# mLSTM cell and a cosine-gated MLP on one core: the model dimension cut into 128, 128 and 64 rows, and what comes with it

## The chip, the cores and the metric

The kernel runs on one core of one Trainium2 chip. A core has five engines that this text names as the profile does: PE (TensorE, matrix multiplication; PEld is its weight load), DVE (VectorE), ACT (ScalarE), POOL (GpSimd) and SP (SyncE, which here only issues DMAs). Each engine works through its own queue in order. The metric is the device time of one execution in microseconds; lower is better.

## What is computed

An mLSTM cell over 4 batches, 8 heads, 768 time steps and head dimension 40, and then an MLP of 320 to 2048 to 320 whose activation is h cos h. Cut to its core:

```python
for t in range(S):                     # batch b, head h
    m_new  = maximum(f[t] + m, i[t])
    f_stab = exp(f[t] + m - m_new); i_stab = exp(i[t] - m_new); m = m_new
    C = f_stab * C + i_stab * outer(v[t], k[t])
    n = f_stab * n + i_stab * k[t]
    y[t] = sigmoid(o[t]) * (C @ q[t]) / maximum(abs(n @ q[t]), 1.0)
x = y.transpose(0, 2, 1, 3).reshape(B * S, H * D)      # 3072 x 320
h = x @ w_in                                           # 320 -> 2048
out = (h * cos(h)) @ w_out                             # 2048 -> 320
```

The inputs q, k, v and the gates are float32. The two weight matrices arrive as float64 and are used as float32.

## The kernel before, in words

Time is cut into 6 blocks (c) of 128 steps. The running maximum m is made up front for all blocks by scans (lines 143 to 173), so that within a block the cell is matmuls. There are 24 **steps** n = 4c + b, one for each block and batch b. A step is `cell(n)` (line 198) and the loads for step n + 3:

- queries and keys are transposed (pt, line 211) and copied from PSUM by ACT and DVE (line 213, `t`);
- the decay matrix E comes by DMA as a row broadcast, DVE subtracts and clamps it head by head (line 218), ACT takes the exponential (line 220);
- scores ps (line 226): heads lie in pairs, one on partitions 0 to 39 and one on 64 to 103, and the first loop does the four even heads, the second the four odd ones; DVE multiplies by E (line 228);
- ph (line 232) is E times the values, with a column of ones for n; pq (line 237) is the query times the state; DVE joins them (hs, lines 240 and 241);
- dn (lines 245 to 247) is the denominator, and two DVE products (249, 250) turn the sigmoid of the output gate, in place, into y; a column scale of 2 pi is taken into dn;
- the state st is updated from pu (lines 254 to 268; POOL makes kw);
- y is transposed (px, line 276) into xT (lines 277 and 280), 320 rows as 120 + 120 + 80.

The MLP runs by block, over the 512 tokens of four batches. `up(c, f)` (line 285) makes one of 16 column blocks of 128: three matmuls (line 289, contraction over 120, 120 and 80 rows) into one of two PSUM banks (`pup`); ACT makes n, the nearest integer of h/2pi + 1/4, by writing int32 (line 293), and h (line 295); DVE takes the difference r straight from PSUM (line 297); ACT takes the sine (line 298); POOL multiplies g = h r (line 300). `down(c, b)` (line 303) sums 16 matmuls over g into po, ACT copies it (line 308) and SP stores it. g has 20 buffers; n, h and r have three each.

The weights are converted in 28 pieces by `to_float32` (line 109): SP fetches the bits, ACT makes the low bits and the absolute high word (118, 120), DVE clamps, shifts and joins the sign (121, 123, 125), POOL adds (126). `weights_in` makes 12 pieces before and between the first four steps (8 of 120 x 512, 4 of 80 x 512); `weights_out` makes 16 pieces of 128 x 320 during the up of block 0. `bits` has three buffers.

The order in the program is: load three steps; four steps with weights_in; then for each block c, four times (four up columns, one step of block c + 1), then four times down. A scheduler reorders each engine's queue within the dependences, so that up, cell and the next block's first up appear interleaved.

PSUM has eight banks: three for `ps_a` (pt, ph, pq, pu, px share them), two for ps, two for pup, one for po.

Of the kernel before, what the change touches and what calls it, by code (L numbers as in the profile page):

```python
# [3 lines left out]

# [7 lines left out]
FP = mybir.dt.float32  # L12
I32 = mybir.dt.int32
U32 = mybir.dt.uint32
AF = mybir.ActivationFunctionType
OP = mybir.AluOpType

LEAST, GREATEST = (struct.unpack("f", struct.pack("I", b))[0] for b in (0x38000000, 0x47EFFFFF))  # L20
TOP2 = -(1 << 30)

TWO_PI = 2.0 * math.pi

TWO_PI_DOWN = 6.28318500518798828125


@with_exitstack
def kernel(
# [20 lines left out]
    nc = tc.nc  # L50

    B, H, S, D = q.shape
    C = 128
# [4 lines left out]
    DM = H * D  # L58
    DFF = moe_w_in.shape[1]
    NF = DFF // 128  # L60

    KH = 3
    cuts = [(h * D, min(h + KH, H) * D) for h in range(0, H, KH)]
    KD = KH * D
    full = DM // KD
    NK = len(cuts)
    NB = 3

    const = ctx.enter_context(tc.tile_pool(name="const", bufs=1))
    wp = ctx.enter_context(tc.tile_pool(name="wp", bufs=1))  # L70
    p2 = ctx.enter_context(tc.tile_pool(name="p2", bufs=2))
    p3 = ctx.enter_context(tc.tile_pool(name="p3", bufs=3))
    dram = ctx.enter_context(tc.tile_pool(name="dram", bufs=1, space=bass.MemoryType.DRAM))
    ps_a = ctx.enter_context(tc.tile_pool(name="ps_a", bufs=3, space=bass.MemoryType.PSUM))
    ps_s = ctx.enter_context(tc.tile_pool(name="ps_s", bufs=1, space=bass.MemoryType.PSUM))
    ps_u = ctx.enter_context(tc.tile_pool(name="ps_u", bufs=2, space=bass.MemoryType.PSUM))
    ps_o = ctx.enter_context(tc.tile_pool(name="ps_o", bufs=1, space=bass.MemoryType.PSUM))


    ident = const.tile([128, 128], FP, name="ident")  # L80
# [2 lines left out]
    nc.gpsimd.memset(late, 0.0)  # L83
    nc.gpsimd.affine_select(out=late, in_=late, compare_op=OP.is_ge, fill=1.0e30, base=0,
                            pattern=[[1, C]], channel_multiplier=-1)
    one = const.tile([BH, 1], FP, name="one")
    nc.vector.memset(one, 1.0)

# [10 lines left out]
    for t in st:  # L99
        nc.gpsimd.memset(t, 0.0)  # L100

    w_in_sb = wp.tile([KD, NK, DFF], FP, name="w_in_sb")
    w_out_sb = wp.tile([128, NF, DM], FP, name="w_out_sb")


    WP = 512
    w_in_bits, w_out_bits = (w.bitcast(I32).rearrange("r (n two) -> r n two", two=2) for w in (moe_w_in, moe_w_out))

    def to_float32(dst, src, eng):
        rows, n = dst.shape  # L110
        r = slice(0, rows)
        bits = p3.tile([128, WP, 2], I32, name="bits", tag="bits")
        eng.dma_start(out=bits[r, 0:n], in_=src)
        hi, lo = bits[r, 0:n, 1], bits[r, 0:n, 0].bitcast(U32)
        t = p2.tile([128, WP], I32, name="wt", tag="wt")[r, 0:n]
        m = p2.tile([128, WP], I32, name="wm", tag="wm")[r, 0:n]

        nc.scalar.activation(out=m, in_=lo, func=AF.Copy, scale=2.0 ** -29)

        nc.scalar.activation(out=t.bitcast(FP), in_=hi.bitcast(FP), func=AF.Abs)  # L120
        nc.vector.tensor_scalar(out=t.bitcast(FP), in0=t.bitcast(FP), scalar1=LEAST, scalar2=GREATEST,  # L121
                                op0=OP.max, op1=OP.min)
        nc.vector.tensor_scalar(out=t, in0=t, scalar1=5, scalar2=2, op0=OP.logical_shift_left,
                                op1=OP.logical_shift_right)
        nc.vector.scalar_tensor_tensor(out=t, in0=hi, scalar=TOP2, in1=t, op0=OP.bitwise_and, op1=OP.bitwise_or)  # L125
        nc.gpsimd.tensor_tensor(out=dst.bitcast(I32), in0=t, in1=m, op=OP.add)

    def weights_in(f):
        for i, (lo, hi) in enumerate(cuts):
            to_float32(w_in_sb[0:hi - lo, i, ts(f, WP)], w_in_bits[lo:hi, ts(f, WP)], nc.sync)  # L130

    def weights_out(f):
        to_float32(w_out_sb[:, f], w_out_bits[ts(f, 128)], nc.sync)


    aT = const.tile([128, NC, BH], FP, name="aT")
# [6 lines left out]
    with tc.tile_pool(name="gates", bufs=1) as gates:  # L143
        f_sb = gates.tile([BH, S], FP, name="f_sb")
        nc.sync.dma_start(out=f_sb, in_=f_gate.rearrange("b h s -> (b h) s"))
        a = gates.tile([BH, S], FP, name="a")
# [31 lines left out]
    sig, xT = {}, {}  # L178
# [19 lines left out]
    def cell(n):  # L198
# [42 lines left out]
            nc.vector.tensor_tensor(out=hs, in0=hs, in1=ph, op=OP.add)  # L241

        dn = p2.tile([128, H], FP, name="dn", tag="dn")

        nc.vector.tensor_scalar(out=dn, in0=hs[:, :, D], scalar1=-TWO_PI, scalar2=TWO_PI, op0=OP.mult, op1=OP.max)
        nc.vector.scalar_tensor_tensor(out=dn, in0=hs[:, :, D], scalar=TWO_PI, in1=dn, op0=OP.mult, op1=OP.max)  # L246
        nc.vector.reciprocal(out=dn, in_=dn)
        y = sig[c][:, b]
        nc.vector.tensor_tensor(out=y, in0=y, in1=hs[:, :, 0:D], op=OP.mult)
        nc.vector.tensor_tensor(out=y, in0=y, in1=dn.unsqueeze(2).to_broadcast([128, H, D]), op=OP.mult)  # L250

        if c < NC - 1:
            kw = p2.tile([128, H, 64], FP, name="kw", tag="kw")
# [15 lines left out]


        if b == 0:
            xT[c] = p2.tile([KD, NK, B, C], FP, name="xT", tag="xT")
        px = ps_a.tile([KD, NK, C], FP, name="px", tag="a")
        yf = y.rearrange("p h d -> p (h d)")
        for i, (lo, hi) in enumerate(cuts):
            nc.tensor.transpose(px[0:hi - lo, i], yf[:, lo:hi], ident)  # L276
        nc.scalar.copy(out=xT[c][:, 0:full, b], in_=px[:, 0:full])  # L277
        for i in range(full, NK):
            r = slice(0, cuts[i][1] - cuts[i][0])
            nc.scalar.copy(out=xT[c][r, i, b], in_=px[r, i])  # L280


    gs = {}

    def up(c, f):
        pu = ps_u.tile([128, B * C], FP, name="pup", tag="up")
        for i, (lo, hi) in enumerate(cuts):
            r = slice(0, hi - lo)
            nc.tensor.matmul(pu, w_in_sb[r, i, ts(f, 128)], xT[c][r, i].rearrange("p b t -> p (b t)"),  # L289
                             start=(i == 0), stop=(i == NK - 1))  # L290

        n = p3.tile([128, B * C], I32, name="n", tag="n")
        nc.scalar.activation(out=n, in_=pu, func=AF.Copy, bias=0.25)  # L293
        h = p3.tile([128, B * C], FP, name="h", tag="h")
        nc.scalar.activation(out=h, in_=pu, func=AF.Copy, scale=TWO_PI)  # L295
        r = p3.tile([128, B * C], FP, name="r", tag="r")
        nc.vector.scalar_tensor_tensor(out=r, in0=pu, scalar=0.25, in1=n, op0=OP.add, op1=OP.subtract)  # L297
        nc.scalar.activation(out=r, in_=r, func=AF.Sin, scale=TWO_PI_DOWN)  # L298
        g = gp.tile([128, B * C], FP, name="g", tag="g")
        nc.gpsimd.tensor_tensor(out=g, in0=h, in1=r, op=OP.mult)  # L300
        gs[c, f] = g
# [24 lines left out]
    for n in range(max(B, NW)):  # L326
        if n < NW:
            weights_in(n)
        if n < B:
            step(n)  # L330
    for c in range(NC):
        for b in range(B):
            for f in range(b * NF // B, (b + 1) * NF // B):
                up(c, f)
                if c == 0:
                    weights_out(f)
            if c + 1 < NC:
                step((c + 1) * B + b)
        for b in range(B):
            down(c, b)  # L340
# [30 lines left out]
```

## Time and profile before

| | |
|---|---|
| median of three runs | 742.99 us (742.42 to 745.64) |
| profiled execution | 742.42 us, of it 740.1 us from the first to the last instruction |
| PE busy | 657.0 us (89%), 2714 matmul instructions |
| PEld busy | 427.9 us (58%) |
| DVE busy | 328.6 us (44%) |
| ACT busy | 316.5 us (43%) |
| POOL busy | 221.9 us (30%) |
| mean granted TensorE clock | 0.977 of full speed |

In the profile a line "L289 PE MATMUL pup<-xT,w_in_sb" names the line of the program, the engine, the operation, and what is written from what. Behind the bar stand the busy time, the mean of one in ns, and the idle time of the engine just before, with what ended it. A float32 matmul of the program is two matmul instructions in the profile. Durations of neighbours on one engine overlap where the engine pipelines them.

### The profile page before, as it was taken

How to read it: one execution, taken by the hardware profiler on the slowest of the kernel's cores; microseconds unless marked ns; L12 is line 12 of the kernel's file. 1: busy time of each engine (PE TensorE's matmuls, PEld its weight loads, DVE VectorE, ACT ScalarE, POOL GpSimd, SP SyncE). 2: the span in 40 equal slices, each digit the busy share in tenths (PEclk: the TensorE clock that was granted, in tenths of full speed). 3: DMA queues.
4: the chain of work that ended last, by engine and by line, in shares of the span. 5: the costliest groups of instructions: out<-in, count | busy, mean ns of one | idle time of the engine just before them, and what ended most of it. 6: DMA issues, size and time to landing. Idle time of an engine off the chain costs nothing.

```text
span 740.1 us, 7672 instructions
## 1 busy us (share of the span) xinstructions
PE 657.0 (89%) x2714; PEld 427.9 (58%) x2714; DVE 328.6 (44%) x726; ACT 316.5 (43%) x529; POOL 221.9 (30%) x213
## 2 busy tenths in 40 slices
PE   4075679889999999999999999999999999999998
PEld 3064545537665555665565665556765566664465
DVE  4178887896601666502656502665402444002200
ACT  4163346863524555433544423555223634026600
POOL 8023455453312333502323502333102322004400
PEclk9999998996999999999989999999899999999999
DMA  9797763341211222311212311211201100000000
GB/s 129 101 210 159 145 171 99 72 127 38 65 46 26 50 52 56 84 34 27 56 39 55 85 34 27 56 50 46 62 18 27 37 1 1 18 19 0 1 18 18
DMA packets 65244, 43.60 MB, mean 59 GB/s; under 512 B 53176, under 2 KB 57208, under 8 KB 65208
## 3 DMA queue, kind: packets, MB, share of 16 engines
q1 hardware_dynamic: 62088, 35.17, 20.3%
q0 software_dynamic: 3072, 7.87, 5.6%
q8 instruction: 21, 0.34, 0.2%
q14 instruction: 15, 0.12, 0.1%
q10 hardware_dynamic: 48, 0.10, 0.0%
HBM read 39.09 MB, written 4.03 MB: 58 GB/s over the span
## 4 chain that ended last, share of the span: by engine, by line
PE 73%; DVE 16%; issue 6%; ACT 3%; DMA 2%; POOL 0%; SPq 0%; DVEq 0%; ACTq 0%
PE po L306 27%; PE pup L289 25%; PE ph L232 8%; PE ps L226 4%; PE pu L257 3%; DVE E L218 3%; PE pq L237 3%; DVE dn L246 3%; PE pt L211 2%; DVE E L228 2%; DVE o L250 1%; PE px L276 1%; DVE st L268 1%; DVE wt L125 1%; DVE wt L121 1%
## 5 line engine op out<-in xcount | busy, mean ns | idle before, releaser
L289 PE MATMUL pup<-xT,w_in_sb 120*128 120x512 f32 (+1 forms) x576 | 269.5, 610 | 4.8 <-DVE r L297 4.8
L300 POOL TENSOR_TENSOR g<-h,r 128x512 f32<-128x512 f32 x96 | 122.8, 1284 | 330.0 <-ACT r L298 312.9
L306 PE MATMUL po<-w_out_sb,g 128*128 128x320 f32 x768 | 216.0, 435 | 2.5 <-ACT o_sb L308 1.5
L306 PEld LDWEIGHTS po<-w_out_sb,g 128*128 128x128 f32 x768 | 144.4, 191 | 67.0 <-ACT o_sb L308 10.2
L289 PEld LDWEIGHTS pup<-xT,w_in_sb 120*128 120x128 f32 (+1 forms) x576 | 107.7, 195 | 121.2 <-issue 97.1
L297 DVE SCALAR_TENSOR_TENSOR r<-pup,n 128x512 f32<-128x512 f32 x96 | 65.7, 687 | 214.0 <-ACT h L295 212.9
L293 ACT ACTIVATE n<-pup 128x512 int32<-128x512 f32 x96 | 57.0, 594 | 109.1 <-PE pup L289 107.0
L218 DVE SCALAR_TENSOR_TENSOR E<-E,aT,late 128x128 f32<-128x128 f32 x192 | 78.6, 470 | 23.2 <-DMA E<-M_d 23.2
L232 PE MATMUL ph<-vs,E 128*128 128x41 f32 x384 | 61.6, 318 | 27.3 <-issue 21.8
L232 PEld LDWEIGHTS ph<-vs,E 128*128 128x128 f32 x384 | 58.2, 231 | 35.0 <-issue 23.7
L298 ACT ACTIVATE r<-r 128x512 f32<-128x512 f32 x96 | 59.8, 635 | 42.4 <-DVE r L297 42.1
L308 ACT COPY o_sb<-po 128x320 f32<-128x320 f32 x24 | 10.2, 424 | 139.5 <-PE po L306 122.8
L295 ACT ACTIVATE h<-pup 128x512 f32<-128x512 f32 x96 | 56.9, 593 | 0.0
L226 PEld LDWEIGHTS ps<-t,t 40*128 40x128 f32 x384 | 42.8, 216 | 23.9 <-ACT t L213 10.4
L226 PE MATMUL ps<-t,t 40*128 40x128 f32 x384 | 47.7, 316 | 8.9 <-DVE t L213 6.8
L193 POOL DMA_DIRECT2D vs<-in_v_dram x24 | 22.1, 923 | 101.6 <-PE pu L257 90.6
L228 DVE TENSOR_TENSOR E<-ps,E 128x512 f32<-128x512 f32 x48 | 31.3, 687 | 22.4 <-PE ps L226 22.3
L276 PE MATMUL px<-ident,o 128*120 128x128 f32 (+1 forms) x72 | 13.6, 303 | 27.9 <-DVE o L250 27.9
L213 DVE COPY t<-pt 128x512 f32<-128x512 f32 x24 | 16.6, 690 | 47.6 <-PE pt L211 47.6
L277 ACT COPY xT<-px 120x256 f32<-120x256 f32 x24 | 8.8, 368 | 53.8 <-PE px L276 53.6
L220 ACT ACT_TABLE_LOAD x20 | 25.7, 1283 | 14.0 <-DMA E<-M_d 13.7
L276 PEld LDWEIGHTS px<-ident,o 128*120 128x120 f32 (+1 forms) x72 | 8.2, 141 | 40.6 <-issue 31.6
(65 smaller groups left out, 531.8 us busy)
## 6 DMA issues: line engine op xcount, KB each, us to landing
E<-M_d SPq DMA_DIRECT2D x24, 512.0 KB, 3.8
bits<-in_moe_w_out_dram SPq DMA_DIRECT2D x16, 320.0 KB, 3.3
qs<-in_q_dram SPq DMA_DIRECT2D x24, 160.0 KB, 3.2
ks<-in_k_dram SPq DMA_DIRECT2D x24, 160.0 KB, 3.5
vs<-in_v_dram POOLq DMA_DIRECT2D x24, 160.0 KB, 3.8
o<-in_o_gate_dram POOLq DMA_DIRECT2D x24, 160.0 KB, 4.2
bits<-in_moe_w_in_dram SPq DMA_DIRECT2D x8, 480.0 KB, 5.8
out_dram<-o_sb SPq DMA_DIRECT2D x24, 160.0 KB, 1.8
```

The source lines that it names most:

```text
L218: nc.vector.scalar_tensor_tensor(out=E[:, h], in0=E[:, h], scalar=aT[:, c, b * H + h:b * H + h + 1], in1=late, op0=OP.subtract, op1=OP.max)
L226: nc.tensor.matmul(ps[:, p], kT[r, p], qT[r, p], start=True, stop=True)
L228: nc.vector.tensor_tensor(out=w, in0=ps, in1=w, op=OP.mult)
L232: nc.tensor.matmul(ph[:, h], E[:, h], vs[i][:, h], start=True, stop=True)
L276: nc.tensor.transpose(px[0:hi - lo, i], yf[:, lo:hi], ident)
L289: nc.tensor.matmul(pu, w_in_sb[r, i, ts(f, 128)], xT[c][r, i].rearrange("p b t -> p (b t)"), start=(i == 0), stop=(i == NK - 1))
L293: nc.scalar.activation(out=n, in_=pu, func=AF.Copy, bias=0.25)
L295: nc.scalar.activation(out=h, in_=pu, func=AF.Copy, scale=TWO_PI)
L297: nc.vector.scalar_tensor_tensor(out=r, in0=pu, scalar=0.25, in1=n, op0=OP.add, op1=OP.subtract)
L298: nc.scalar.activation(out=r, in_=r, func=AF.Sin, scale=TWO_PI_DOWN)
L300: nc.gpsimd.tensor_tensor(out=g, in0=h, in1=r, op=OP.mult)
L306: nc.tensor.matmul(po, gs[c, f][:, ts(b, C)], w_out_sb[:, f], start=(f == 0), stop=(f == NF - 1))
```

## The change

- **Contraction.** The 320 rows are cut into 128, 128 and 64. `up` makes two column blocks at once: four matmuls over 128 rows, then two over 64 rows, the one on partitions 0 to 63, the other on 64 to 127. For that the last 64 rows of w_in are stored twice as narrow (`w_in_l`: even column blocks on the lower half, odd ones on the upper), and y carries its last 64 columns twice, so that px (now three whole transposes) puts them on both halves.
- **PSUM.** ps_a has two banks (three before), pup three (two before).
- **Activation.** h is copied from PSUM; n is rounded by adding and subtracting a large constant on ACT; DVE subtracts 2 pi n from h in two parts and clamps; ACT takes the absolute value and sin(pi/2 - |r|). Three ACT operations become five, one DVE operation becomes three, and DVE reads SBUF instead of PSUM.
- **Denominator.** The scale of 2 pi is gone; y is a tile of its own instead of the gate's.
- **Weights.** The conversion takes exponent, sign and mantissa apart: seven DVE operations a piece instead of three on DVE and two on ACT; the fetch is issued by POOL instead of SP. The pieces are 10 of 128 x 512 and 16 of 128 x 320; those of w_in_l are fetched by two DMAs.

```diff
-    ps_a = ctx.enter_context(tc.tile_pool(name="ps_a", bufs=3, space=bass.MemoryType.PSUM))
+    ps_a = ctx.enter_context(tc.tile_pool(name="ps_a", bufs=2, space=bass.MemoryType.PSUM))
...
-    ps_u = ctx.enter_context(tc.tile_pool(name="ps_u", bufs=2, space=bass.MemoryType.PSUM))
+    ps_u = ctx.enter_context(tc.tile_pool(name="ps_u", bufs=3, space=bass.MemoryType.PSUM))
...
-        eng.dma_start(out=bits[r, 0:n], in_=src)
+        for part, s in src:
+            eng.dma_start(out=bits[part, 0:n], in_=s)
...
-        nc.scalar.activation(out=m, in_=lo, func=AF.Copy, scale=2.0 ** -29)
-
-        nc.scalar.activation(out=t.bitcast(FP), in_=hi.bitcast(FP), func=AF.Abs)
-        nc.vector.tensor_scalar(out=t.bitcast(FP), in0=t.bitcast(FP), scalar1=LEAST, scalar2=GREATEST,
-                                op0=OP.max, op1=OP.min)
-        nc.vector.tensor_scalar(out=t, in0=t, scalar1=5, scalar2=2, op0=OP.logical_shift_left,
-                                op1=OP.logical_shift_right)
-        nc.vector.scalar_tensor_tensor(out=t, in0=hi, scalar=TOP2, in1=t, op0=OP.bitwise_and, op1=OP.bitwise_or)
-        nc.gpsimd.tensor_tensor(out=dst.bitcast(I32), in0=t, in1=m, op=OP.add)
+        nc.vector.tensor_scalar(out=t, in0=hi, scalar1=20, scalar2=0x7FF, op0=OP.logical_shift_right,
+                                op1=OP.bitwise_and)
+        nc.vector.tensor_scalar(out=t, in0=t, scalar1=float(REBIAS), scalar2=float(REBIAS + 254), op0=OP.max, op1=OP.min)
+        nc.vector.tensor_scalar(out=t, in0=t, scalar1=float(REBIAS), scalar2=float(1 << 23), op0=OP.subtract, op1=OP.mult)
+        nc.vector.scalar_tensor_tensor(out=t, in0=hi, scalar=SIGN, in1=t, op0=OP.bitwise_and, op1=OP.bitwise_or)
+
+        nc.vector.tensor_scalar(out=m, in0=hi, scalar1=TOP, scalar2=3, op0=OP.bitwise_and, op1=OP.logical_shift_left)
+        nc.vector.tensor_tensor(out=m, in0=m, in1=t, op=OP.bitwise_or)
+        t, m = t.bitcast(FP), m.bitcast(FP)
+        nc.vector.scalar_tensor_tensor(out=t, in0=lo, scalar=2.0 ** -52, in1=t, op0=OP.mult, op1=OP.mult)
+        nc.gpsimd.tensor_tensor(out=dst, in0=m, in1=t, op=OP.add)
...
-        nc.vector.tensor_tensor(out=y, in0=y, in1=dn.unsqueeze(2).to_broadcast([128, H, D]), op=OP.mult)
+        y = p2.tile([128, 2 * DM - KL], FP, name="y", tag="y")
+        yh = y[:, 0:DM].rearrange("p (h d) -> p h d", h=H)
+        nc.vector.tensor_tensor(out=yh, in0=sig[c][:, b], in1=hs[:, :, 0:D], op=OP.mult)
+        nc.vector.tensor_tensor(out=yh, in0=yh, in1=dn.unsqueeze(2).to_broadcast([128, H, D]), op=OP.mult)
+        nc.vector.tensor_copy(out=y[:, DM:], in_=y[:, KL:DM])
...
+        px = ps_a.tile([128, NK + 1, C], FP, name="px", tag="a")
+        for i in range(NK + 1):
+            nc.tensor.transpose(px[:, i], y[:, ts(i, 128)], ident)
+        nc.scalar.copy(out=xT[c][:, :, b], in_=px)
...
+        for e, pu in enumerate(pair):
+            for i in range(NK):
+                nc.tensor.matmul(pu, w_in_sb[:, i, ts(2 * f2 + e, 128)], x(i), start=(i == 0), stop=False)
+        for e, pu in enumerate(pair):
+            r = slice(64 * e, 64 * e + 64)
+            nc.tensor.matmul(pu, w_in_l[r, f2], x(NK, r), start=False, stop=True)
+        for e, pu in enumerate(pair):
+            act(c, 2 * f2 + e, pu)
...
-        n = p3.tile([128, B * C], I32, name="n", tag="n")
-        nc.scalar.activation(out=n, in_=pu, func=AF.Copy, bias=0.25)
         h = p3.tile([128, B * C], FP, name="h", tag="h")
-        nc.scalar.activation(out=h, in_=pu, func=AF.Copy, scale=TWO_PI)
+        nc.scalar.copy(out=h, in_=pu)
+        n = p3.tile([128, B * C], FP, name="n", tag="n")
+        nc.scalar.activation(out=n, in_=h, func=AF.Identity, scale=INV_2PI, bias=magic)
+        nc.scalar.activation(out=n, in_=n, func=AF.Identity, bias=unmagic)
         r = p3.tile([128, B * C], FP, name="r", tag="r")
-        nc.vector.scalar_tensor_tensor(out=r, in0=pu, scalar=0.25, in1=n, op0=OP.add, op1=OP.subtract)
-        nc.scalar.activation(out=r, in_=r, func=AF.Sin, scale=TWO_PI_DOWN)
+        nc.vector.scalar_tensor_tensor(out=r, in0=n, scalar=-TWO_PI_HI, in1=h, op0=OP.mult, op1=OP.add)
+        nc.vector.scalar_tensor_tensor(out=r, in0=n, scalar=-TWO_PI_LO, in1=r, op0=OP.mult, op1=OP.add)
+        nc.vector.tensor_scalar(out=r, in0=r, scalar1=math.pi, scalar2=-math.pi, op0=OP.min, op1=OP.max)
+        nc.scalar.activation(out=r, in_=r, func=AF.Abs)
+        nc.scalar.activation(out=r, in_=r, func=AF.Sin, scale=-1.0, bias=half_pi)
```

In the changed kernel the 128-row matmuls of up stand in line 308, the 64-row ones in line 311, the three DVE operations in lines 323 to 325, and the weights in lines 128 to 138.

## The prediction

> **What bounds the kernel now.** I read the page from the top: the busy shares, the 40 slices, the chain that ended last, the groups. Then the trace's windows by stage, and the chain in order of time.
>
> ```profile
> PE 73%; DVE 16%; issue 6%; ACT 3%; DMA 2%; POOL 0%; SPq 0%; DVEq 0%; ACTq 0%
> ```
>
> TensorE carries 73% of the chain, VectorE 16%, so TensorE bounds the whole. But the whole is an average. The windows, one row a stage (length; busy PE, weight load, DVE, ACT, POOL; clock; DMA):
>
> ```profile
> 0.00:40.00 40.00, 8.86 (x45) 7.42 (x46) 14.73 (x69) 12.29 (x20) 15.38 (x34) 1.00 0.87 125
> 40.00:106.00 66.00, 43.44 (x189) 38.33 (x189) 51.65 (x114) 28.38 (x49) 29.36 (x25) 1.00 0.76 164
> 106.00:202.00 96.00, 85.99 (x358) 54.21 (x357) 74.02 (x147) 59.44 (x101) 42.20 (x40) 0.89 0.34 88
> ...
> 339.30:450.50 111.20, 106.73 (x461) 68.97 (x461) 49.19 (x104) 48.82 (x78) 31.91 (x28) 0.97 0.20 49
> ...
> 661.40:700.00 38.60, 38.60 (x91) 16.96 (x91) 9.69 (x14) 24.36 (x43) 16.47 (x13) 1.00 0.01 5
> ```
>
> Up to 202 us (first cells, weight conversion, up of block 0) VectorE is as full as TensorE: 125.7 us busy in the 162 us from 40 to 202. From 230 us on TensorE is 96% busy and VectorE under half. At 661.4 to 700 the last up runs alone, TensorE without a gap: 90 instructions, 0.43 us each. A matmul over 512 columns is two of them, 0.86 us, whether it contracts 120 rows or 80.
>
> The chain in one steady step (cell plus four up columns):
>
> ```profile
> 459.95 1.14 PE ps L226 x11
> ...
> 466.49 1.50 DVE dn L246
> ...
> 469.77 6.88 PE pup L289 x16
> 476.65 0.88 PE pt L211 x8
> 477.52 1.62 PE po L306 x6
> ```
>
> The step repeats every 20.0 us (ps at 459.95, the next at 479.96): about 11 us through the cell, where VectorE's answers count, the rest matmuls.
>
> **The change, part by part.** All is summed onto the profiled execution, 742.42 us (span 740.1 us and 2.3 us around it); the median of the runs is 742.99 us.
>
> *1. Matmuls.* A pair of column blocks costs 6 x 0.86 = 5.16 us now. After, it is four 128-row matmuls (3.44 us) and two 64-row ones. Do 64-row halves run side by side? The score matmuls L226 are such halves (rows 0 and 64). Counted in half microseconds of one cell:
>
> ```profile
> 459.94:460.44 0.50, 0.49 (x4) 1.00 0.92 164
> 460.44:460.94 0.50, 0.50 (x10) 1.00 1.25 207
> 460.94:461.44 0.50, 0.50 (x9) 1.00 1.14 159
> ```
>
> Rows count what overlaps a window, so neighbours share one. While only the first half has work there are 4, when both have, 10: they run together. So two 64-row matmuls take 0.86 us, not 1.72. But going into such a mode costs:
>
> ```profile
> 499.48 0.59 PE L289 MATMUL pup<-xT,w_in_sb 120*128 120x512 f32 x1
> 500.00 0.37 PE L226 MATMUL ps<-t,t 40*128 40x128 f32 x1
> ```
>
> 0.52 us from start to start where 0.43 is the rhythm: 0.09 us. I count 0.09 on the way back too. A pair side by side is 3.44 + 0.86 + 0.18 = 4.48 us, 0.68 less. [...]
>
> The scheduled order of the changed kernel decides how often it comes true. Only 28 of 48 pairs have the two 64-row matmuls next to each other; in 20 another 128-row matmul (ph, px, po, the next column block) stands between. A split pair costs up to 3.44 + 1.72 + 0.36 = 5.52 us, 0.36 more. TensorE in all: 28 x 0.68 - 20 x 0.36 = 11.8 us less. px, three transposes as before: nothing.
>
> *2. Element-wise work of up, 96 columns.*
>
> ```profile
> L300 POOL TENSOR_TENSOR g<-h,r 128x512 f32<-128x512 f32 x96 | 122.8, 1284 | 330.0 <-ACT r L298 312.9
> L297 DVE SCALAR_TENSOR_TENSOR r<-pup,n 128x512 f32<-128x512 f32 x96 | 65.7, 687 | 214.0 <-ACT h L295 212.9
> L293 ACT ACTIVATE n<-pup 128x512 int32<-128x512 f32 x96 | 57.0, 594 | 109.1 <-PE pup L289 107.0
> ```
>
> ScalarE: three operations (0.59 + 0.59 + 0.64 = 1.82) become five; those on SBUF I price like L298, 0.63: 0.59 + 3 x 0.63 + 0.64 = 3.12 us, +1.30. VectorE: L297 (0.69) becomes two of that kind and a tensor_scalar of 0.42 (fastest rows of L121 and L123 at 512): 1.80 us, +1.11. But L297 reads PSUM; the new ones read n and h from SBUF, as GpSimd's g does. The trace has such a meeting:
>
> ```profile
> 78.91 2.49 POOL L126 TENSOR_TENSOR w_in_sb<-wt,wm 120x512 int32<-120x512 int32 x2
> 79.19 2.37 DVE L218 SCALAR_TENSOR_TENSOR E<-E,aT,late 128x128 f32<-128x128 f32 x1
> ```
>
> An operation whose median is 0.35 us stood until GpSimd was done. L297 beside g never does: its 96 lie between 0.675 and 0.693. So VectorE and GpSimd follow one another: 1.80 + 1.27 = 3.07 us a column. [...]
>
> Stage 339.3 to 450.5: 27.7 us at its end are down, 83 us are left for four cells and 16 columns. VectorE 49.2 + 16 x 1.11 = 67 us; GpSimd's tensor operations 16 x 1.27 + 4 x 1.05 = 24.5; of VectorE's, some 15 us read PSUM (t, E<-ps, hs, st<-pu) and can hide GpSimd's. So 77 to 92 us, against 83, and ScalarE 48.8 + 16 x 1.30 = 70 of 111. TensorE's gain there is 2 us, covered up. Each column passes ACT, DVE, ACT, POOL, and h (three buffers) waits for g three columns back, so a late g holds ScalarE, a held ScalarE holds the PSUM bank, and the cell's matmuls queue behind the pup that waits. The two banks of ps_a (three before) let pu wait for pq's reader: 0 to 1.8 us a step, one column's VectorE work. I take 90 us of 83 for the stage: +7, four stages (230 to 661): **+28 us**. Ends: -8 (only TensorE's gain) and +60 (a step of 23.7 us).
>
> *3. Weights.* 28 pieces become 26 (10 of 512 columns, 16 of 320), each with seven VectorE operations, and none on ScalarE (31.6 us go, from a ScalarE with half its time free: nothing). A 512 piece: four tensor_scalar at 0.42 (fastest) to 0.70 (mean of L123 at 120x512), three two-input ones at 0.68: 3.7 to 4.9 us; I take 4.1. A 320 piece, 0.32 to 0.55 and 0.48 to 0.52: 2.7 to 3.8; I take 3.1. Sum 41 + 50 = 91 us for 45 now (L121, L123, L125): +46, less some 14 where neighbours overlap by 0.08: +32 (ends +22 and +63). It all lies before 202 us, with block 0's up (16 x 1.11 = 18) and eight 64-column copies (0.2 each): VectorE there needs 125.7 + 52 = 178 us after 40 us. At 78% busy, as now, it ends at 268; without a gap at 218. I take 90%, since conversions wait for nothing but their DMA: 238, **+36 us**. Ends +15 and +60. The 28 weight DMAs move from SP's queue to GpSimd's: 28 x 0.92 (vs L193) = 26 us on an engine with 115 of 202 us free: nothing, as long as three bits buffers cover 5.8 us to landing; each waits behind a conversion's last add. The queries' DMAs on SP no longer stand behind weights: gain nothing, they wait for their buffer.
>
> *4. Last up.* 15 columns at 38.6 us now; after, VectorE plus GpSimd 3.07 or ScalarE 3.12 a column: 15 x 3.12 = 46.8, and about 1 us until g is ready: **+9 us** (ends +3, if neighbours overlap, and +14).
>
> *5. Small.* dn: one two-input operation for another of 8 columns, nothing (at most 1.5 us a cell both ways, the row of L246). The copy of 64 columns of y is on the path to nothing but px: 0.2 x 24 = 5 us if nothing covered it; px of its columns stands in the queue behind earlier ones; counted in 2.
>
> Sum: 742.4 + 28 + 36 + 9 = **815 us**.
>
> **Rivals.**
> - *Everything is covered* (ends faster). Mechanism: TensorE stays last in every stage. For it: 330 us of idle before g on GpSimd, 214 before L297. It decides if the VectorE-GpSimd pair needs under 83 us a stage and conversions fit the 36 us idle between 40 and 202. 742.4 - 11.8 = 731 us. Against it: +52 us do not fit 36. 5%.
> - *Only the start pays.* The pair stays near 80 us a stage: 742.4 + 20 + 0 + 4 = 766. For it: PSUM readers can hide most of g. 17%, of it 2% within 0.5% of now.
> - *The queues feed on each other.* Three busy in-order engines: a step takes 25 us: 16 x 5 = 80, and 36 + 14: 872 us. For it: a column's way has four handovers and three buffers. 17%.
> - *The halves do not run side by side* (the change fails at its name), because of the semaphore waits between them: 28 x 0.86 = 24 us on TensorE, of which a third shows, since it is not last in the steps: 823 us. 6%.
> - The forecast, 815 us: 55%.
>
> **Numbers.** Range 756 to 878 us: from below the second case to above the third, leaving out the covered case and the upper part of the third, 13 to 20%. Half a percent is about what a measurement of this kernel can tell from no change. Faster by more than that 5%, within 2%, slower 93%.
>
> **What would show it.** In the changed profile: L311 pairs with starts 0.43 us apart in twos; L323 longer than 0.7 us when g runs; VectorE over 85% busy until about 240 us; steps of about 22 us with pup waiting for ACT h; the last up near 47 us. I am wrong if VectorE's share stays below 60% in the steps while TensorE stays at 96%, or if L323 is never stretched.

## The result, and the profile after

| | before | after |
|---|---|---|
| median | 742.70 us (737.22 to 745.64) | 883.38 us (876.98 to 885.01) |
| ratio, 95% interval | | 1.189 (1.180 to 1.198) |
| profiled execution, span | 742.42, 740.1 us | 885.01, 883.2 us |
| PE / DVE / ACT / POOL busy | 657 / 329 / 317 / 222 us | 742 / 510 / 407 / 255 us |
| mean granted clock | 0.977 | 0.872 |

815 us was forecast, with a range to 878; the changed kernel is slower than that. Intervals of ratios compare only runs within 1.5% of the fastest of their kernel; medians are over all runs.

The same windows by stage in the changed kernel (length; busy PE, weight load, DVE, ACT, POOL; clock; DMA share and GB/s). The third answers to 339.3 to 450.5 of before, the last to 661.4 to 700:

```profile
40.00:120.00 80.00, 41.72 (x185) 36.92 (x186) 64.65 (x144) 10.78 (x14) 35.99 (x36) 1.00 0.43 118
120.00:240.00 120.00, 94.33 (x324) 53.42 (x324) 107.00 (x231) 66.65 (x99) 63.38 (x51) 0.77 0.26 68
...
412.20:543.90 131.70, 122.20 (x461) 75.43 (x460) 74.03 (x140) 68.56 (x104) 32.36 (x28) 0.86 0.17 42
788.00:833.00 45.00, 39.44 (x94) 13.51 (x93) 28.11 (x38) 38.51 (x65) 14.70 (x12) 0.96 0.01 4
```

Read the third row beside that of before: the stage is 20.5 us longer (131.7 for 111.2), but TensorE is not idle in the difference. Its busy time rose by 15.5 us for the same 461 matmuls, and the clock column fell from 0.97 to 0.86. The chain that ended last, which carried the first reading of before, follows only the last 4% here and says nothing of the stages:

```profile
PE 3%; ACT 1%; DVE 0%; POOLq 0%; issue 0%; ACTq 0%; DVEq 0%
```

The page's clock row, 40 slices in tenths, before and then after:

```profile
PEclk9999998996999999999989999999899999999999
```

```profile
PEclk9999997878579679789678989779789789999979
```

At 5 half of the rate was granted all through the slice. At half of the rate the small matmuls of a cell (L250, L255, L276) start 213 ns apart in the median; at the full rate, 112.

The first 9s of both rows are no measurement. The record of the clock begins with its first change, at 105.9 us before and at 123.7 us after. Ahead of that the page counts the full rate, but the matmuls stand 213 ns apart in all 17 kernels of this text, which is the rhythm of half of it. The chain of before shows it, two of its lines (start, length; the first ahead of the first record):

```profile
40.93 2.93 PE ph L232 x14
...
243.89 1.53 PE ph L232 x14
```

**A sum that closes.** The trace gives every stretch at half clock from its first record on, so each span can be split: *work* (TensorE's busy time with half of that at half clock taken off), *clock* (that half) and *idle*. It is an identity, but it tests itself: seven kernels with the matmuls of before have busy times from 655 to 715 us, and a work of 638.2 to 642.4. By stages (each ends where its fourth copy of po begins, the last at the end of the span), us:

| stage | length before, after | work | clock | idle |
|---|---|---|---|---|
| to down of block 0 | 230.1, 280.7 | 156.2, 158.6 | 10.2, 25.8 | 63.7, 96.4 |
| four middle blocks | 431.3, 507.3 | 409.9, 408.5 | 6.8, 71.2 | 14.7, 27.5 |
| last block | 78.6, 95.3 | 73.9, 72.9 | 0.0, 5.1 | 4.7, 17.2 |
| all | 740.1, 883.2 | 640.0, 640.1 | 17.1, 102.1 | 83.0, 141.1 |

Of the 143 us, 85 are the clock, 58 are waits, and nothing came off the work. This is an account, not yet a price: if one term were smaller, the others could grow. The half clock ahead of the first record is counted as work in these rows, some 26 us in both kernels. Counted as clock it makes 613.9 and 613.3 us of work, 43.2 and 128.9 of clock, so the difference stays. The first record lies at 97 to 127 us in all kernels but one (`after_warm`, 62 us), so the differences below change by less than 2 us, but for that one, where it is taken up.

The groups of up in the changed kernel (busy, mean ns; idle before):

```profile
L329 POOL TENSOR_TENSOR g<-h,r 128x512 f32<-128x512 f32 x96 | 133.5, 1392 | 386.6 <-ACT r L327 384.9
L323 DVE SCALAR_TENSOR_TENSOR r<-n,h 128x512 f32<-128x512 f32 x96 | 78.2, 817 | 210.9 <-ACT n L321 210.7
L326 ACT ACTIVATE r<-r 128x512 f32<-128x512 f32 x96 | 59.8, 625 | 61.4 <-DVE r L325 60.6
L324 DVE SCALAR_TENSOR_TENSOR r<-n,r 128x512 f32<-128x512 f32 x96 | 85.9, 898 | 1.6
L320 ACT ACTIVATE n<-h,magic 128x512 f32<-128x512 f32 x96 | 68.0, 715 | 0.9
```

In order of time (start, duration), VectorE and then GpSimd:

```profile
481.13 1.68 DVE L324 SCALAR_TENSOR_TENSOR r<-n,r 128x512 f32<-128x512 f32 x1
482.74 0.68 DVE L323 SCALAR_TENSOR_TENSOR r<-n,h 128x512 f32<-128x512 f32 x1
```

```profile
480.99 1.27 POOL L329 TENSOR_TENSOR g<-h,r 128x512 f32<-128x512 f32 x1 [3.70 <-ACT r L327]
```

L324 stands while g runs (to 482.26) and ends 0.55 us after it; the next L324, which meets no g, takes 0.68 in all (at 483.68). The two take turns, as forecast. And the pairs, on TensorE:

```profile
472.02 1.13 PE L311 MATMUL pup<-xT,w_in_l 64*128 64x512 f32 x4
```

Four matmuls of some 0.6 us in 1.13: they start in twos, 7 ns apart inside a two (0.43 had been forecast between the twos, it is 0.53).

### The profile page after: what moved, and what is told of

It reads as the page before. It is cut to its first block, busy times and chain, and to the rows that moved or that the text cites. A ratio compares the mean times of both kernels' runs of the same rounds, so it can differ in the third digit from the quotient of the medians.

```text
span 883.2 us, 8083 instructions
## 1 busy us (share of the span) xinstructions
PE 742.2 (84%) x2714; PEld 457.8 (52%) x2714; DVE 510.0 (58%) x1043; ACT 407.0 (46%) x630; POOL 255.4 (29%) x239
## 5 line engine op out<-in xcount | busy, mean ns | idle before, releaser
L308 PE MATMUL pup<-xT,w_in_sb 128*128 128x512 f32 x384 | 207.3, 672 | 6.1 <-ACT h L318 6.1
L323 DVE SCALAR_TENSOR_TENSOR r<-n,h 128x512 f32<-128x512 f32 x96 | 78.2, 817 | 210.9 <-ACT n L321 210.7
L250 PE MATMUL ph<-vs,E 128*128 128x41 f32 x384 | 77.7, 371 | 59.2 <-issue 31.6
L308 PEld LDWEIGHTS pup<-xT,w_in_sb 128*128 128x128 f32 x384 | 76.5, 215 | 92.5 <-issue 68.2
L250 PEld LDWEIGHTS ph<-vs,E 128*128 128x128 f32 x384 | 72.7, 282 | 80.3 <-DVE E L246 38.6
L311 PE MATMUL pup<-xT,w_in_l 64*128 64x512 f32 x192 | 91.4, 730 | 0.0
L324 DVE SCALAR_TENSOR_TENSOR r<-n,r 128x512 f32<-128x512 f32 x96 | 85.9, 898 | 1.6
L318 ACT COPY h<-pup 128x512 f32<-128x512 f32 x96 | 55.4, 577 | 60.8 <-PE pup L311 34.0
L337 ACT COPY o_sb<-po 128x320 f32<-128x320 f32 x24 | 10.2, 424 | 153.3 <-PE po L335 153.3
L320 ACT ACTIVATE n<-h,magic 128x512 f32<-128x512 f32 x96 | 68.0, 715 | 0.9
L327 ACT ACTIVATE r<-r,half_pi 128x512 f32<-128x512 f32 x96 | 68.2, 713 | 0.6
L321 ACT ACTIVATE n<-n,unmagic 128x512 f32<-128x512 f32 x96 | 68.1, 712 | 0.4
L244 PE MATMUL ps<-t,t 40*128 40x128 f32 x384 | 48.7, 319 | 19.0 <-ACT t L231 10.2
L244 PEld LDWEIGHTS ps<-t,t 40*128 40x128 f32 x384 | 43.5, 218 | 35.1 <-ACT t L231 20.1
L211 POOL DMA_DIRECT2D vs<-in_v_dram x24 | 22.4, 933 | 126.5 <-PE pu L276 112.5
L325 DVE TENSOR_SCALAR r<-r 128x512 f32<-128x512 f32 x96 | 45.8, 479 | 1.5
```

What stands on the lines that cost most here:

```text
L244: nc.tensor.matmul(ps[:, p], kT[r, p], qT[r, p], start=True, stop=True)
L250: nc.tensor.matmul(ph[:, h], E[:, h], vs[i][:, h], start=True, stop=True)
L308: nc.tensor.matmul(pu, w_in_sb[:, i, ts(2 * f2 + e, 128)], x(i), start=(i == 0), stop=False)
L311: nc.tensor.matmul(pu, w_in_l[r, f2], x(NK, r), start=False, stop=True)
L320: nc.scalar.activation(out=n, in_=h, func=AF.Identity, scale=INV_2PI, bias=magic)
L321: nc.scalar.activation(out=n, in_=n, func=AF.Identity, bias=unmagic)
```

## The experiments

All ratios are against runs of the kernel before on the same chip. In the expectations, theory A is that the element-wise work of up and of the weights makes the loss, B that the pairs do, C that the parts hurt only together, D that the longer chain does by waits and by the clock that falls with them.

**One part at a time.** `m_only`: before with the pairs, the banks and y; `act_only`: before with the new activation and denominator; `w_only`: before with the new conversion on POOL's queue.

```diff
 # act_only (two lines of the activation of the change, in the loop of before)
-        nc.vector.scalar_tensor_tensor(out=r, in0=pu, scalar=0.25, in1=n, op0=OP.add, op1=OP.subtract)
+        nc.vector.scalar_tensor_tensor(out=r, in0=n, scalar=-TWO_PI_HI, in1=h, op0=OP.mult, op1=OP.add)
...
 # w_only
-            to_float32(w_in_sb[0:hi - lo, i, ts(f, WP)], w_in_bits[lo:hi, ts(f, WP)], nc.sync)
+            to_float32(w_in_sb[0:hi - lo, i, ts(f, WP)], w_in_bits[lo:hi, ts(f, WP)], nc.gpsimd)
```

> The kernel before with the matmul part alone: 128, 128 and 64 rows, pairs side by side, two ps_a and three pup banks, y with doubled columns; activation, denominator scale and weight conversion as before. In its scheduled order nearly all pairs have their 64-row matmuls next to each other. Theory A (the element-wise work of up makes the loss in the steps and the last up, the weights the loss at the start): TensorE gains up to 48 x 0.68 = 33 us, so 710 to 738 us. Rival B (the pairs make the loss: two of three banks at once, split halves, two ps_a banks): 790 us or more.

> The kernel before with the changed activation alone (five ScalarE and three VectorE operations, VectorE reading SBUF, and the plain denominator). Theory A: the four middle blocks lose about 76 us and the last up 16 us, as in the changed kernel, so 815 to 845 us. Rival B: under 765 us. Rival C (only the parts together load the queues enough): 765 to 800 us.

> The kernel before with the changed weight conversion alone, fetched by GpSimd's queue. Theory A: the start loses some 40 to 50 us, the later blocks nothing, so 780 to 795 us. Rival C: the start alone hides it in VectorE's 36 us of idle time: under 760 us.

| | median us (before 736.9) | ratio, 95% | work | clock | idle |
|---|---|---|---|---|---|
| m_only | 749.3 | 1.014 (1.007 to 1.021) | 619.6 | 37.0 | 90.2 |
| act_only | 826.8 | 1.122 (1.117 to 1.127) | 641.7 | 73.2 | 108.7 |
| w_only | 772.0 | 1.050 (1.045 to 1.054) | 640.1 | 15.4 | 112.3 |

The activation makes +90 us, the weights +35, the pairs +12: 137 of the 141 between the medians (the pairs' 12 is 5 to 15 by its interval). So B falls, and C with it as far as single parts go. A was right for the activation, 8 us high for the weights, and wrong for the pairs: they take 20 us of work off TensorE and still do not make it faster.

**Undo the activation.** `after_act_before`: the changed kernel with the activation of before.

```diff
-        nc.scalar.activation(out=n, in_=h, func=AF.Identity, scale=INV_2PI, bias=magic)
-        nc.scalar.activation(out=n, in_=n, func=AF.Identity, bias=unmagic)
...
+        nc.scalar.activation(out=n, in_=pu, func=AF.Copy, bias=0.25)
```

> The changed kernel with the activation of before, so pairs and weight conversion only. If the parts add up (35 us for the weights, 7 to 10 for the pairs): 775 to 795 us. If the activation hurts most together with the other parts (theory C): 755 to 772 us. Work at full clock near 620 us where the pairs stay side by side, near 640 where the order splits them.

766.1 us, 1.037 (1.029 to 1.044); work 622.1, clock 20.1, idle 119.2. This lies where theory C put it: pairs and weights together cost 27, alone 12 and 35, and without the new activation 117 us go, more than the 90 it adds alone; 82 of the 122 us of span are clock. All but one pair run side by side, in the changed kernel 28 of 48: the new activation also spoils the order of the pairs.

**Where in the activation.** `before_sbuf`: the one VectorE operation reads h in SBUF. `before_act2`: two more ScalarE operations. `before_dve3`: two more VectorE operations. `after_psum`: the changed kernel with the first of the three reading the product in PSUM.

```diff
 # before_sbuf
-        nc.vector.scalar_tensor_tensor(out=r, in0=pu, scalar=0.25, in1=n, op0=OP.add, op1=OP.subtract)
+        nc.vector.scalar_tensor_tensor(out=r, in0=h, scalar=1.0 / TWO_PI, in1=n, op0=OP.mult, op1=OP.subtract)
...
+        nc.scalar.activation(out=r, in_=r, func=AF.Sin, scale=TWO_PI_DOWN, bias=quarter)
 # before_act2, ahead of the sine
+        nc.scalar.activation(out=r, in_=r, func=AF.Identity, bias=zero)
+        nc.scalar.activation(out=r, in_=r, func=AF.Identity, bias=zero)
 # before_dve3, ahead of the sine
+        nc.vector.scalar_tensor_tensor(out=r, in0=n, scalar=0.0, in1=r, op0=OP.mult, op1=OP.add)
+        nc.vector.tensor_scalar(out=r, in0=r, scalar1=1.0, scalar2=-1.0, op0=OP.min, op1=OP.max)
 # after_psum
-        nc.vector.scalar_tensor_tensor(out=r, in0=n, scalar=-TWO_PI_HI, in1=h, op0=OP.mult, op1=OP.add)
+        nc.vector.scalar_tensor_tensor(out=r, in0=n, scalar=-TWO_PI_HI, in1=pu, op0=OP.mult, op1=OP.add)
```

> The kernel before, but the one VectorE operation of up reads h from SBUF (h/2pi - n) in place of the product in PSUM; the quarter turn goes into the sine as a bias. Same number of operations on every engine. If VectorE and GpSimd taking turns at SBUF makes a large part of the activation's 90 us (theory A): L297's mean goes from 0.69 to over 1.2 us, some of the 96 stand over 1.9 us, and the time is 765 to 800 us. If the turns cost little while VectorE has room (theory D, the longer chain through ScalarE): the operation is stretched all the same, but the time stays at 735 to 752 us.

> The kernel before with two more ScalarE operations a column of up (r plus zero, twice, ahead of the sine; the constant is an operand, as in the changed kernel). They add 2 x 0.71 x 96 = 136 us of ScalarE and about 1.4 us to each column's way; VectorE is as before. If ScalarE's longer chain makes a large part of the activation's 90 us (theory D): 770 to 800 us, and more waits for h and the banks of pup. If only VectorE and GpSimd matter (theory A): 735 to 752 us.

> The kernel before with two more VectorE operations a column on SBUF (r plus zero times n, and a clamp that changes nothing), as many as the changed activation has; ScalarE's three operations as before. Together with the two more ScalarE operations (27 to 32 us) it is nearly the changed activation (87 to 90 us). If the shares add up, 785 to 805 us, with the two-input operation on SBUF stretched to over 0.9 us in the mean. If the operations hurt only together with ScalarE's longer chain: 745 to 765 us.

> The changed kernel, in which the first VectorE operation of a column reads h from its PSUM bank instead of the copy in SBUF, so that one of three VectorE operations cannot meet GpSimd's product any more; the bank is held longer. Theory A in the form that the shared access of VectorE and GpSimd to SBUF makes the loss: 96 x up to 0.7 us less, 845 to 870 us. Rival D (the loss is the longer chain of operations with its waits, and TensorE's clock that falls in the gaps): 878 us or more.

| | median us | ratio, 95% | clock | idle |
|---|---|---|---|---|
| before_sbuf | 744.5 | 1.007 (1.003 to 1.010) | 20.4 | 81.4 |
| before_act2 | 769.5 | 1.043 (1.037 to 1.048) | 34.4 | 96.0 |
| before_dve3 | 782.8 | 1.062 (1.054 to 1.070) | 34.7 | 101.8 |
| after_psum | 867.1 | 1.178 (1.172 to 1.183) | 74.8 | 137.7 |

The operation of before_sbuf meets g and is stretched less than theory A said (mean 766 ns for 687, longest 1520):

```profile
L299 DVE SCALAR_TENSOR_TENSOR r<-h,n 128x512 f32<-128x512 f32 x96 | 73.5, 766 | 221.1 <-ACT h L297 220.3
```

So taking turns costs at most 5 us by itself (the sine of this kernel also takes 0.72 us in place of 0.63, since its bias is an operand). Two ScalarE operations cost 30, two VectorE operations 44: 79 of the activation's 90. The 44 are not free of turns either: the added two-input operation meets g and takes 0.76 us in the mean, for which over 0.9 had been expected. before_sbuf and before_act2 came out as theory D said (the latter half a microsecond below its range), before_dve3 2 us below the range for shares that add up. No single share explains the 90, and the turns by themselves explain the least of them. The waits more than add up (-2, 13 and 19 us against 26), the clock does not get there (3 + 17 + 18 = 38 against 56).

after_psum came out against this: 16 us faster than the changed kernel, in the range of theory A (845 to 870) and not of rival D (878 or more). Its L323 takes 0.69 us at most, where that of the changed kernel takes up to 1.76. By the split the gain in span, 19.5 us, is 27 us of clock and 3 of idle time, less 11 us of work (only 20 of 48 pairs stay together, 28 in the changed kernel). So in the changed kernel the turns of one operation do cost, mostly by way of the clock; the order of the pairs and the time that a bank is held change with it, so its share is not isolated.

**Why the pairs win nothing.** `m_first`: m_only with the 64-row products ahead. `m_banks`: m_only with po in the cell's banks, three again. `m_samehalf`: m_only with both 64-row products on rows 0 to 63.

```diff
 # m_first: ahead of the four products over 128 rows
+            nc.tensor.matmul(pu, w_in_l[r, f2], x(NK, r), start=True, stop=False)
 # m_banks
-        po = ps_o.tile([128, DM], FP, name="po", tag="o")
+        po = ps_a.tile([128, DM], FP, name="po", tag="a")
 # m_samehalf
-            r = slice(64 * e, 64 * e + 64)
+            r = slice(0, 64)
```

> The kernel with only the pairs of column blocks (activation and weights as before), but with the two 64-row products ahead of the four 128-row ones, so that the two banks of a pair are finished 1.7 us apart and not together. If the gain of the pairs was lost because both banks fall due at once (theory: banks): 718 to 738 us, and less waiting of ACT n for pup. If it was lost to the clock or to the cell's two PSUM banks: 743 to 756 us, as with the 64-row products last.

> The kernel with only the pairs, and po taken from the cell's banks of PSUM, which are three again instead of two and one. If the gain of the pairs (20 us of TensorE's work) is lost because the cell has two banks (theory: banks): 715 to 737 us, less idle time and less half clock. If it is lost to the pair's own two banks of pup or to the clock alone: 743 to 756 us, as with only the pairs. If po in the cell's banks holds the cell up: above 760.

> The kernel with only the pairs, but both 64-row products on rows 0 to 63, so that they cannot run side by side (odd column blocks then take the 64 rows of weights and of y that belong to even ones). If side by side is where the pairs' gain comes from: TensorE's work at full clock rises from 620 to 655 to 662 us (47 pairs by 0.86 us), and the time from 749 to 775 to 800 us. If not: 745 to 756 us.

| | median us | ratio, 95% | work | clock | idle |
|---|---|---|---|---|---|
| m_first | 756.4 | 1.027 (1.019 to 1.035) | 634.8 | 37.1 | 81.4 |
| m_banks | 822.8 | 1.115 (1.108 to 1.121) | 622.4 | 84.9 | 113.6 |
| m_samehalf | 749.7 | 1.011 (1.006 to 1.016) | 656.7 | 23.6 | 71.9 |

Both forecasts on banks missed, but neither kernel tests the banks alone. In m_first the order no longer puts the halves together (20 pairs of 48). In m_banks po competes with the cell for its banks; ScalarE's wait for pup goes from 112.5 to 155.1 us. So it stays open whether the banks hold the gain back. m_samehalf tells more: no halves side by side, TensorE's work 37 us up as forecast, and the time that of m_only (medians 749.7 and 749.3 us). Their totals, m_only and then m_samehalf:

```profile
PE 656.6 (88%) x2714; PEld 415.4 (56%) x2714; DVE 330.4 (44%) x744; ACT 305.8 (41%) x500; POOL 218.2 (29%) x211
```

```profile
PE 680.3 (90%) x2714; PEld 426.2 (57%) x2714; DVE 334.9 (45%) x744; ACT 306.0 (41%) x500; POOL 217.8 (29%) x211
```

The busy time differs by 24 us, the profiled spans by 5 (746.8 and 752.2 us). What TensorE saves comes back in m_only as 18 us of idle time and 13 of clock. TensorE at 88% "busy" was not what set the pace of these steps; what did is not isolated by any run here.

**Is the clock a cause?** First, what its changes follow in these profiles. In the records of before and after the clock reads 1.0 or 0.5 and nothing else, and the time between two changes is always a whole number of stretches of 3.41 us. Cut the profile into these stretches, and add up in each the columns that TensorE streams, as time (0.43 us for 512, from each matmul's start on), weighted by rows used out of 128. Over 17 profiles, from 100 us on, at the full clock: 161 of the 184 falls follow a stretch with under 1.25 us (the others lie between 1.25 and 1.39), and 2723 of the 2725 stretches that end without a fall have 1.25 or more. At half clock: 188 of 189 rises follow a stretch with 1.25 or more, and 312 of the 336 that end without a rise have less. Without the weight by rows they mix: only 69 of the 184 falls lie under 1.25, and others reach 2.99. In act_only, without the weight, falls follow stretches with up to 2.37 us and none follows others with 1.26; weighted, its 13 falls lie at 1.23 or less and the 152 others at 1.26 or more. Long gaps do not tell the falls from the rest: two of the 184 follow a stretch that was idle throughout, and 80 follow one without a gap of 1 us; in the changed kernel the longest gap in the two stretches ahead of a fall is 0.2 to 3.4 us, in 17 of 21 under 1.9. Nor does the busy time: from 710.79 to 714.20 us of the changed kernel TensorE is "busy" for 3.12 of 3.41 us, 22 of its 24 matmuls there are a cell's, over 40 rows or over 41 or 82 columns, the row-weighted sum is 1.13 us, and the clock of the next stretch is 0.50; from 205.59 to 209.00 us it is busy for 1.55, the sum is 1.38, and the clock stays at 1.00.

In the four middle blocks of the changed kernel 39 of 147 stretches have under 1.25 us of that sum, in before 2 of 125. The stretches ahead of the 15 falls there hold 0.36 us of up and down in the mean, where the mean of all is 1.82; 0.67 us are the cell's small matmuls, and TensorE is idle for 0.99.

Then three kernels that change it. `after_warm`: ten products over 128 columns, whose results nobody reads, ahead of ph in each step of the changed kernel. `after_thin`: the same over 32 rows. `m_warm0`: m_only with them in steps 4 to 7 alone.

```diff
+        for _ in range(10):
+            nc.tensor.matmul(pw[:, 384:512], ident, late, start=True, stop=True)
 # after_thin
+            nc.tensor.matmul(pw[:, 384:512], ident[0:32], late[0:32], start=True, stop=True)
```

> The changed kernel with 10 useless products over 128 columns in each step, between the scores and ph, to keep TensorE at work while it waits for VectorE's E; they are about 10 x 2 x 0.107 = 2.1 us a step or 51 us in all at the full clock. If the falling clock makes a large part of the loss (theory D): time at half clock falls from 226 us to under 140 us and the kernel takes 845 to 875 us although TensorE has 51 us more to do. If the clock only follows the waits and costs little: 880 to 930 us.

> The same useless products in the same order as in the kernel with 10 of them a step, of the same length, but over 32 rows in place of 128. If the clock goes by how many rows of the array are at work in a stretch of 3.41 us, and it costs time (theory D): time at half clock goes back from 177 to 200 us or more, and the kernel is slower by half the difference, 893 to 912 us. If the clock goes by idle time alone, or costs nothing: 177 us at half clock and 877 to 888 us, as with 128 rows.

> The kernel with only the pairs, and 10 useless products over 128 columns in each of the four steps that run beside the weights (steps 4 to 7), where 48 of its 77 us at half clock lie: at most 4 x 2.1 = 9 us more work, and up to 24 us won if the clock stays up. Theory D: 730 to 742 us, half clock before 237 us under 30 us. If the clock only follows the waits there: 747 to 760 us.

| | median us | ratio, 95% | half clock, us | work | clock | idle |
|---|---|---|---|---|---|---|
| after | 883.4 | 1.189 (1.180 to 1.198) | 226 | 640.1 | 102.1 | 141.1 |
| after_warm | 882.4 | 1.195 (1.187 to 1.202) | 177 | 674.3 | 75.2 | 132.8 |
| after_thin | 921.8 | 1.242 (1.237 to 1.247) | 208 | 698.7 | 96.9 | 124.4 |
| m_only | 749.3 | 1.014 (1.007 to 1.021) | 77 | 619.6 | 37.0 | 90.2 |
| m_warm0 | 743.9 | 0.999 (0.995 to 1.003) | 28 | 631.7 | 13.7 | 89.2 |

These rows count from the first record of the clock on, and after_warm's comes early: its clock first rises at 62 us, that of the other two at 124 and 127. With the half clock ahead of the first record counted as such:

| | first record, us | half clock, us | work | clock | idle |
|---|---|---|---|---|---|
| after | 123.7 | 349 | 613.3 | 128.9 | 141.1 |
| after_warm | 62.1 | 237 | 662.0 | 87.5 | 132.8 |
| after_thin | 127.2 | 333 | 662.5 | 133.1 | 124.4 |

after_warm by itself tells little: 49 us more work, 41 less of clock, 8 less idle, and no time won (theory D had hoped for under 140 us at half clock in the recorded part, and it is 177). after_thin does: each engine's order is the same, only the rows differ, the work is the same within 0.5 us, and the clock takes 45.6 us more. Two groups of after_warm, and the same of after_thin:

```profile
L253 PE MATMUL ph<-vs,E 128*128 128x41 f32 x384 | 64.9, 333 | 43.2 <-DVE E L246 43.1
L244 PE MATMUL ps<-t,t 40*128 40x128 f32 x384 | 43.9, 298 | 12.6 <-DVE t L231 8.2
```

```profile
L253 PE MATMUL ph<-vs,E 128*128 128x41 f32 x384 | 77.4, 375 | 41.8 <-DVE E L246 41.8
L244 PE MATMUL ps<-t,t 40*128 40x128 f32 x384 | 51.4, 331 | 10.1 <-DVE t L231 6.6
```

The waits ahead of ph are the same, its matmuls are not. after_thin's span is 37.8 us longer: 45.6 of clock and 0.5 of work, less 8.4 idle. So here most of what the clock takes is paid. It is 10 us slower than theory D said, which went by the recorded half clock; 23.9 of the 45.6 us lie ahead of the first records. m_warm0 wins back what was expected of the clock before 237 us (7 us at half clock there in place of 48); its median is 2 us above the forecast, its twelve times lie in two groups, 735 to 737 and 744 to 752. It is the fastest kernel with the pairs and no better than before.

**One that told nothing.** `before_late`: E of the odd heads is multiplied by 1 twice more.

```diff
+        for _ in range(2):
+            nc.vector.tensor_scalar(out=w, in0=w, scalar1=1.0, scalar2=1.0, op0=OP.mult, op1=OP.mult)
```

> The kernel before, in which VectorE multiplies half of E by 1 twice more in each step, before TensorE may begin ph: 2 x 0.42 = 0.84 us later, 24 times, 20 us in all. If TensorE's clock makes an idle time cost more than itself (theory D): TensorE's idle time rises by 10 to 20 us, its time at half clock from 36 to over 80 us, its work at full clock stays at 640 us, and the kernel takes 765 to 785 us. If only the wait itself counts: at most 20 us more, 745 to 762 us, at an unchanged clock.

751.0 us in the median, 12 above the 738.9 of before, but ten times from 733 to 760; the ratio, 0.996 (0.990 to 1.002), rests on the three below 738. The profiled execution took 752.4 us: work 642.4, clock 21.6, idle 86.4. Its 3 us more of idle time and 5 more of clock are too few to show a price.

## Why the prediction was wrong, by its own steps

1. **Matmuls, -11.8.** Measured 0 (work 640.0 and 640.1). The 28 adjacent pairs came true (56 starts within 50 ns of another), and the halves run side by side. But in the changed kernel, at the full clock, it is 0.52 us from the start of a 128-row matmul to that of the first two, 0.53 between the twos, and 0.52 from the second two to the next 128-row matmul (medians), where 0.43 is the rhythm. That is 0.09, 0.1 and 0.09 more, which leaves 0.58 of the 0.86; m_only's 47 pairs gave 0.43 each (20.4 / 47), not 0.68. The last 0.15 I could not place. For 28 that is 12, so the 20 split ones cost some 0.6 each (an estimate from the two), not 0.36.
2. **Steps, +28. This is the step that failed.** Measured +76. The waits in it were about right, even high: idle time of the four blocks rose by 12.8. Its mechanism came true too (L324 held by g; VectorE 74.0 and ScalarE 68.6 us a stage where 67 and 70 were priced). What the sum has no term for is TensorE's clock: it takes the rates of before as given for every stage, though the clock column stood among its rows (0.97 in the steady stage). In these blocks the clock took 71.2 us where it had taken 6.8, +64 us without one matmul more. So the 0.97 was no constant of the kernel. ScalarE's operations with a constant as operand took 0.71, not 0.63, which makes the chain 0.25 us longer a column.
3. **Weights, +36.** Measured +50.6, of which idle 32.7, clock 15.6, work 2.4. VectorE's 92 us for the conversions (91 priced) and its 107 of 120 us (89%, 90 taken) were right; the remainder is the clock again. w_only, where the clock did not fall further (15.4 us against 17.1), cost the 35 us that were forecast.
4. **Last up, +9.** 45.0 us where 47 was forecast. The last block in all grew by 16.7: idle 12.5, clock 5.1.
5. **Small terms.** Not separable in these runs.

So 73 us of waits were forecast and 58 came; 85 of clock were not forecast. The rival that came nearest, queues that feed on each other at 872 us, did so for another reason: it asked for 80 us of waiting in the steps, and there are 13. The test I set ("wrong if VectorE's share stays below 60% in the steps while TensorE stays at 96%") was half met: VectorE 56%, TensorE 93%, and L323 and L324 stretched.

What is shown: the parts' prices, the sum, that 37 us of TensorE's work are all but covered in the kernel with the pairs alone (m_samehalf), that the same products over 32 rows in place of 128 bring 333 us at half clock for 237 in the changed kernel, and a span 37.8 us longer (after_thin, after_warm), that the clock takes 73.2 us with the new activation (act_only) and 20.1 without it (after_act_before), and that up and down are nearly missing from the stretches ahead of its falls (0.36 us where the mean is 1.82). What is argued: that they are missing because the activation's later answers pull the big matmuls of up away from the cell's small ones. No run changed that order alone. The 27 us by which the activation hurts more in the changed kernel (117) than in before (90) is also only placed (clock and split pairs), not tested.

## What to carry to other kernels

Split a span into TensorE's work, half of its time at half clock, and idle time, and ask of a change what it does to each: here 58 us of waits came with 85 us of clock. Look at the rhythm of the matmuls too, not at the clock's row alone: here the row shows the full rate until the first change is recorded, at 105.9 us before and 123.7 after, while the matmuls start 213 ns apart. A high busy share of TensorE is no proof that it sets the pace: test that by giving it more to do. In the kernel with the pairs alone, where it is 88% busy, 37 us more work cost next to nothing, in the changed kernel 46 us more at half clock cost 38. And a rounding trick that saves nothing on the busiest engine but adds two operations on each of two engines cost 90 us, though in the changed kernel's steps neither of the two is busy for more than about 56% of the time.

## What was unexpected of the hardware

- Of 184 falls of the clock to a half in 17 profiles, 161 follow a stretch of 3.41 us with under 1.25 us (37%) of streaming weighted by rows, the others one with 1.25 to 1.39; ahead of one fall in the changed kernel the longest gap was 0.2 us. Ten products a step over 128 rows (after_warm) and ten over 32 (after_thin), in the same order, gave 237 and 333 us at half clock.
- At the start the matmuls stood 213 ns apart, the rhythm of half the rate, up to the clock's first record at 97 to 127 us in 16 of 17 kernels, while the page's row shows the full rate; with the ten products over 128 rows (after_warm) the first rise came at 62 us.
- ScalarE's sine over 128 x 512 takes 0.72 us with a bias that is an operand (before_sbuf), without one 0.63 (before).
- Two 64-row float32 matmuls on the two halves start 7 ns apart, and the next two 0.53 us later, where 0.43 had been forecast (after, L311).
